# Output projection in paired 64-row pieces, constant matmuls in the opening, and another order of the opening loads

## The chip, the cores and the metric

The kernel runs on one core of one Trainium2 chip. The metric is the device time of one execution in microseconds, lower is better. The core has a matrix engine (TensorE, PE in the profile; its weight loads are listed apart as PEld), a vector engine (DVE), a scalar engine (ACT), GpSimd (POOL), and SyncE (SP), whose queue here issues every transfer (DMA). Matmul results go to PSUM, which has 8 banks of 512 fp32 columns.

## The reference, cut to what matters

```python
# x: (1, 2048, 576), bf16;  wqkv: (576, 1728);  wo: (576, 576)
# w_gate, w_up: (576, 4608);  w_down: (4608, 576)
xn = layernorm(x)
q, k, v = split(xn @ wqkv)                      # 32 heads of 18
p = softmax(where(0 <= i - j < 256, q @ k.T * 18 ** -0.5, -1e9))
s = (p @ v) @ wo                                # the output projection
h = sigmoid(xn @ w_gate) * (xn @ w_up)
out = x + s * silu(h @ w_down)
```

## The kernel before, in words

The 2048 tokens are worked in four chunks `c` of 512 (`CH`), each of four blocks of 128 (`QPC`). A chunk goes through these stages:

- `build_ln` loads the x blocks, normalises them (two `bn_stats`, `bn_aggr`, an add, a power on POOL, one `tensor_scalar`, a 64-column wrap copy) and turns them over into `xn`: in chunk 0 by PE transposes (L403, nine to a block) and an ACT copy (L412), in later chunks by DMA. The feature dimension of 576 lies there as nine slabs of 64, each in both halves of the 128 rows, in a shifted order, so that two matmuls of 64 rows can run side by side in the upper and the lower half of the array. The program calls this mode `r64`.
- `build_qkv` makes q, k and v of each block with `project` (L416): nine slabs by two halves, 18 matmuls of 288 columns (L423). The order in chunk 0 is the string `QKV_FIRST`. A q or k result is copied to a slot of `pk` (three slots, `RPK`) and turned over into `qkp` by a DMA transpose (`qkt`, L462); a slot is free again when that transpose has landed, so the fourth q or k projection waits for the first transpose, and so on.
- `build_attn` does the scores (L505), exponentials (L527), masks (L561) and p·v (L584) for eight groups of four heads. `after_pv` divides, turns over, and writes `op_`; DMAs named `oc` (L618 to L628) gather 18-row pieces of `op_` into `oT`, whose rows are the contraction of the output projection.
- `build_wo` (L630) is the output projection: per block five row tiles (four of 126 rows, one of 72), each against 512 and 64 columns of `wo_sb`: ten matmuls a block, 40 a chunk (L642), each block into its own pair of PSUM banks. ACT copies the result to `sat` (L650).
- `build_ffn`: gate and up, 36 tiles `ft` of 128 features (`fa`, `fb`: L678, `r64`, 18 matmuls of 512 columns each; the two last up-matmuls of a tile are carried into the next tile's `fa`), tanh on ACT (L664), product on DVE (L668). The weights come in groups of three tiles, four DMAs a group (`load9`), into a ring of three slots (`RW`). Then the down projection (L746 and, in the last block, L776): 128-row matmuls of 512 and 64 columns in turn, in pieces of four tiles `q`.

The order of every engine's program is computed by `schedule` (L819): a list scheduler takes, per engine, the operation with the smallest start time plus `prio` times 40 ns, by durations and a transfer model that are written in the source. Operations with `prio` 1 (projections, output projection) so go ahead of those with `prio` 3 (gate/up and down) where both can start. An operation that writes PSUM names candidate banks (`Psum`): the output projection pairs (4, 5), (6, 7), (0, 1), (2, 3); gate and up one bank each of 4 to 7; the down projection one of the same pairs. It can be placed only where all users of the earlier tenant have been placed. All transfers are issued by SP, in that static order, each behind its own waits. `emit` writes semaphore waits between engines; between two PE operations it writes none.

In chunk 0 SP issues the four x blocks, then 12 parts of `wqkv` (q, k, v, four each), three parts of the first gate/up group, three q/k transposes, the fourth part, and so on.

## Time and profile before

| what | value |
|---|---|
| median of 3 runs (lowest, highest) | 580.01 us (579.92, 580.15) |
| the profiled execution: time / span | 580.4 us / 578.4 us |
| PE busy in the span | 564.7 us (98%), 6185 matmuls |
| gate and up (L678) | 2592 matmuls, 299.4 us busy |
| down (L746) | 1080 matmuls, of which the trace has 1053 |
| q, k, v (L423) | 864 matmuls, 56.4 us busy |
| output projection (L642) | 160 matmuls: 64 of 126 rows by 512 columns, 64 of 126 by 64, 16 of 72 by 512, 16 of 72 by 64 |
| transposes of chunk 0 (L403) | 36 matmuls of 128 columns |
| first matmul | 6.75 us after the start of the span |
| DMA | 72.73 MB, 126 GB/s in the mean; 248 GB/s from 5 to 10 us, 236 from 10 to 15 us |

The span is the time from the first to the last instruction of the profiled execution; the 2.0 us to its own time lie around it. A matmul's duration in the profile runs from its start to a modelled end, and matmuls overlap: what one costs is the distance from its start to the next one's start. Rows of groups give durations; starts are read from the timeline.

### The profile page before, as it was taken

What the parts mean: (1) busy time and instruction counts of PE and PEld (TensorE: products, weight loads), DVE (VectorE), ACT (ScalarE), POOL (GpSimd) and SP (SyncE); (2) the same over time, 40 slices, a digit from 0 to 9 for tenths busy, and PEclk for the clock granted to TensorE, in tenths of its full rate; (3) what the DMA queues carried; (4) which work ended last, traced back from release to release, by engine and by line L of the source; (5) the groups of instructions that cost most, each with busy time, mean ns of one, the idle gap of its engine ahead of it and who ended that gap; (6) DMA issues with size and microseconds to landing.
All of it is one profiled execution on the core that took longest, in us unless ns stands there. A gap on an engine that the chain in (4) does not pass through costs nothing.

```text
span 578.4 us, 14464 instructions
## 1 busy us (share of the span) xinstructions
PE 564.7 (98%) x6185; PEld 274.1 (47%) x6212; DVE 295.0 (51%) x588; ACT 304.5 (53%) x411; POOL 25.0 (4%) x51
## 2 busy tenths in 40 slices
PE   5999999999999999999999999999999999999997
PEld 3654334457544444445754444444564444444554
DVE  4247988403157887611226697751312677774112
ACT  5357887214168787530337788732133878873101
POOL 3001110000000010000000011000000000000000
PEclk9999999999999999999999999999999999999999
DMA  8999999624946665313793556432389355651010
GB/s 202 203 191 231 216 223 199 160 44 92 210 93 134 145 155 127 80 44 82 106 210 92 139 132 158 111 90 46 69 167 185 73 124 136 134 126 39 1 42 20
DMA packets 124091, 72.73 MB, mean 126 GB/s; under 512 B 53157, under 2 KB 123525, under 8 KB 124029
## 3 DMA queue, kind: packets, MB, share of 16 engines
q1 hardware_dynamic: 124029, 71.82, 58.8%
q8 instruction: 49, 0.80, 0.6%
q14 instruction: 13, 0.11, 0.1%
HBM read 55.15 MB, written 2.36 MB: 99 GB/s over the span
## 4 chain that ended last, share of the span: by engine, by line
PE 97%; DVE 1%; DMA 1%; issue 0%; ACT 0%; SPq 0%
PE ps L678 50%; PE ps L746 23%; PE ps L423 9%; PE ps L505 5%; PE ps L584 4%; PE ps L642 3%; PE ps L776 2%; DMA xr<-in_A_x_dram 1%; PE ps L403 1%; ACT sat L650 0%; DVE bnst L367 0%; DVE bnst L369 0%; DVE xnr L380 0%; DVE mv L371 0%; SPq L193 0%
## 5 line engine op out<-in xcount | busy, mean ns | idle before, releaser
L678 PE MATMUL ps<-xn,wgs 64*128 64x512 bf16 x2592 | 299.4, 377 | 0.0
L527 ACT ACTIVATE expr<-ps 128x1024 bf16<-128x1024 f32 (+2 forms) x192 | 175.8, 968 | 39.9 <-PE ps L505 39.2
L678 PEld LDWEIGHTS ps<-xn,wgs 64*128 64x128 bf16 x2592 | 121.0, 94 | 148.5 <-issue 14.3
L746 PE MATMUL ps<-wd_sb,hT 128*128 128x64 bf16 (+1 forms) x1053 | 131.9, 284 | 2.5 <-issue 1.1
L668 DVE SCALAR_TENSOR_TENSOR hT<-tring,ps 128x512 bf16<-128x512 bf16 x144 | 97.2, 675 | 49.5 <-ACT tring L664 25.1
L664 ACT ACTIVATE tring<-ps 128x512 bf16<-128x512 f32 x144 | 86.3, 599 | 68.7 <-PE ps L678 66.0
L561 DVE TENSOR_TENSOR expr<-expr,m 128x1024 bf16<-128x1024 bf16 (+1 forms) x152 | 82.3, 572 | 60.4 <-ACT expr L527 60.2
L746 PEld LDWEIGHTS ps<-wd_sb,hT 128*128 128x128 bf16 x1080 | 68.1, 98 | 66.4 <-issue 4.4
L807 ACT ACTIVATE thf<-ps 128x576 bf16<-128x576 f32 (+2 forms) x17 | 10.6, 623 | 98.4 <-PE ps L746 90.8
L423 PE MATMUL ps<-wqkv_sb,xn 64*128 64x288 bf16 x864 | 56.4, 286 | 0.0
L809 DVE SCALAR_TENSOR_TENSOR thf<-thf,ps 128x576 bf16<-128x576 bf16 (+2 forms) x17 | 12.2, 719 | 85.4 <-ACT thf L807 85.4
L423 PEld LDWEIGHTS ps<-wqkv_sb,xn 64*128 64x128 bf16 x864 | 42.0, 95 | 13.0 <-issue 1.4
L505 PE MATMUL ps<-qkp 18*128 18x384 bf16 (+2 forms) x704 | 36.8, 276 | 0.0
L457 DVE CAST pk<-ps 128x576 bf16<-128x576 f32 x16 | 12.1, 757 | 48.0 <-PE ps L423 48.0
L599 DVE STREAM_TRANSPOSE tf<-ps 128x512 f32<-128x512 f32 x32 | 22.9, 716 | 13.5 <-PE ps L505 10.4
L505 PEld LDWEIGHTS ps<-qkp 18*128 18x128 bf16 x704 | 11.1, 92 | 34.6 <-issue 20.2
L458 ACT ACTIVATE pk<-ps 128x576 bf16<-128x576 f32 x16 | 10.4, 652 | 31.2 <-PE ps L423 31.2
L566 POOL COPY qkp<-qkp 128x256 bf16<-128x256 bf16 x24 | 12.2, 507 | 313.3 <-PE ps L505 313.3
L584 PE MATMUL ps<-expr,vau 128*32 128x256 bf16 (+2 forms) x704 | 25.6, 277 | 0.0
L613 DVE STREAM_TRANSPOSE op__63<-pk 128x512 bf16<-128x512 bf16 x32 | 22.7, 708 | 0.9 <-DVE pk L607 0.3
L642 PE MATMUL ps<-wo_sb,oT 126*128 126x512 bf16 (+3 forms) x160 | 20.4, 286 | 0.0
L584 PEld LDWEIGHTS ps<-expr,vau 128*32 128x32 bf16 x704 | 13.1, 96 | 15.4 <-ACT tring L664 7.6
(36 smaller groups left out, 141.1 us busy)
## 6 DMA issues: line engine op xcount, KB each, us to landing
wgs<-in_B_w_gate_dram SPq DMA_DIRECT2D x48, 240.0 KB, 3.9
wgs<-in_B_w_up_dram SPq DMA_DIRECT2D x48, 240.0 KB, 4.7
wgs<-in_B_w_up_dram SPq DMA_DIRECT2D x48, 192.0 KB, 4.2
wgs<-in_B_w_gate_dram SPq DMA_DIRECT2D x48, 192.0 KB, 4.8
wd_sb<-in_B_w_down_dram SPq DMA_DIRECT2D x9, 576.0 KB, 6.9
xf<-in_A_x_dram SPq DMA_DIRECT2D x18, 144.0 KB, 2.3
out_dram<-xf SPq DMA_DIRECT2D x15, 144.0 KB, 1.8
xr<-in_A_x_dram SPq DMA_DIRECT2D x14, 144.0 KB, 4.2
```

The lines of the kernel that those rows point to most:

```text
L423: r = e.matmul(self.bank(ps, HV, hf), self.xn[r0:r0 + 64, k, i * P:(i + 1) * P], self.wqkv_sb[r0:r0 + 64, j, k, :], start=(k == 0), stop=( ...
L505: r = e.matmul(self.ps[:, b:b + n * P], self.qkp[r0:r0 + DH, hg, k0:k0 + P], self.qkp[r0:r0 + DH, hg, q0 * P:(q0 + n) * P], start=True, st ...
L527: return e.activation(self.expr[:, es, 2 * pr:2 * pr + 2, 0:nblk * P], src, ACTF.Exp, scale=SM_SCALE)
L561: return e.tensor_tensor(ap, ap, m, ALU.mult)
L584: r = e.matmul(self.ps[32 * j:32 * j + 32, b + q0 * P:b + (q0 + n) * P], vf[:, v0:v0 + 32], self.expr[:, es, j, pos * P:(pos + n) * P], st ...
L599: t1 = self.rd("DVE", dve_ns(CH), lambda e, ps=ps: e.transpose(tf.rearrange("p g d -> p (g d)"), self.bank(ps)), f"t1:{c}:{hg}", deps=[o_p ...
L613: t2 = self.op("DVE", dve_ns(CH), lambda e, on=on: e.transpose(self.op_[:, hg % NOT, :], on.rearrange("p g d -> p (g d)")), f"t2:{c}:{hg}" ...
L642: r = e.matmul(self.ps[:, b + n0:b + n1], self.oT[0:k, kt, qi * P:(qi + 1) * P], self.wo_sb[0:k, kt, n0:n1], start=(kt == 0), stop=(kt == ...
L664: return e.activation(self.tring[:, st_, :], self.bank(ps), ACTF.Tanh, scale=0.5)
L668: return e.scalar_tensor_tensor(self.hT[:, ft, :], self.tring[:, st_, :], 1.0, self.bank(ps), ALU.add, ALU.mult)
L678: return e.matmul(self.bank((pg, pu)[gu][ft]), self.wgs[r0:r0 + 64, slots[ft // FG], i, fl * P:(fl + 1) * P], self.xn[r0:r0 + 64, i, :], s ...
L746: r = e.matmul(self.ps[:, b + n0:b + n1], lhsT, self.wd_sb[:, q, fl, n0:n1], start=(ft == 0), stop=(ft == NFT - 1))
```

## The change

Four things change together.

1. **Output projection.** `oT` and `wo_sb` now hold full tiles of 128 rows in the first four row tiles and the other 64 rows of the contraction in the fifth. In the fifth, the lower 64 rows carry token columns 0 to 255 and the upper 64 rows columns 256 to 511. The matmuls take 64 rows each and go in pairs, one in each half of the array, for two blocks at once: blocks 0 and 2, then 1 and 3. A pair of blocks takes two operations: the first has all five row tiles (20 matmuls), with one block's lower and the other's upper half; the second (16 matmuls, four row tiles) has the halves exchanged. The second adds to banks that the first wrote through the other half of the array, so it gets a real semaphore wait on the first (`fence`), also in the scheduler's model. Each operation holds two pairs of banks. The gather DMAs become 18-row pieces with a rest of 2 rows, and two 16-row pieces of 256 columns for each late head group: 16 `oc` issues a chunk in place of 11; the weight's small pieces become eight of 16 rows in place of four of 18.
2. **Opening on PE.** DVE fills a tile of `hT` with ones first of all; PE runs ten matmuls of 512 columns on it before any data has arrived, and one more after each of the transposes of blocks 0 and 1. Their bank (3) is not read.
3. **Loads.** SP's order in the opening becomes, by the new priorities: x0, x1, q weights, x2, v weights, x3, k weights, the first gate/up group. The layernorm of chunk 0 gets a higher priority for earlier blocks (`LN_STEP`), and the scheduler's estimate of the transfer time of `wqkv` goes from 1.55 to 1.35.
4. **Projections of chunk 0** follow `QKV_FIRST` in its new order, with v next to q. The first one (q0) is split after four slabs, so that its first part needs only the first half of `xn` and two of the four weight parts.

```diff
--- before.py
+++ after.py
...
 NOT = 4
-KO = 7 * DH
+WO_PRIO = 1
 KL = 4 * DH
...
 SKEW = 2
-QKV_FIRST = "q0 k0 q1 k1 q2 k2 q3 k3 v0 v1 v2 v3"
+QKV_FIRST = "q0 q1 v0 v1 q2 v2 k0 v3 k1 q3 k2 k3"
 QKV_NEXT = "q0 k0 q1 v0 v1 k1 q2 k2 v2 q3 k3 v3"
...
 LATE_SLACK = 5000.0
-LN_STEP = 0
+LN_STEP = 1
+WARM = 10
+X0_SLACK = 0.0
+WARM_MORE = (1, 1)
+X_PRIO = (-9, -9, -7, -5)
+QKV_LOAD = (-8, -4, -6)
+W0_PRIO = -3
+WARM_NS = 427.0
+W_FACTOR = 1.35
 XT_BYTES = 1.6
...
                 for o in self.ops:
-                    if o.name.startswith("wo:0:"):
+                    if o.name.startswith("wo:0:") and o.fence is None:
                         o.add_dep(self.op_wo)
...
         self.op_negh = op("DVE", 60, lambda e: e.memset(self.neghalf[:, :], -0.5), "neghalf", prio=0)
+        self.op_pre = op("DVE", 250, lambda e: e.memset(self.hT[:, 0, :], 1.0), "pre", prio=-9)
         id1 = op("POOL", 200, lambda e: e.memset(self.op_[:, NOT - 1, 0:P], 1.0), "id1", prio=0)
...
         self.op_vones = op("POOL", 300, lambda e: e.memset(self.vau[:, :, H, :], 1.0), "vpad", deps=[vo1], prio=1)
+        self.warm(WARM, "warm:0", [self.op_pre])
         self.op_pkz = op("ACT", 1300 + 1900, lambda e: e.memzero(self.pk[:, :, :, :]), "pkz", prio=0)
 
-    def load9(self, low, up, w_low, w_up, name, lane, deps, prio, eng="SP"):
+    def warm(self, n, name, deps, odeps=()):
+        ps = Psum((3,))
+
+        def f(e):
+            for k in range(n):
+                r = e.matmul(self.bank(ps), self.hT[:, 0, 0:P], self.hT[:, 0, :], start=True, stop=True)
+            return r
+        self.op_warm = self.pe(n * WARM_NS, f, name, deps=deps, prio=-9, psum=[ps], odeps=odeps)
+
+    def load9(self, low, up, w_low, w_up, name, lane, deps, prio, factor=1.55):
         cols = w_low.shape[1]
...
                                            (low[:, 5:NC, :], a[:, 1:NC:2, :], 4), (up[:, 4:NC, :], b[:, 0:NC:2, :], 5))):
-            out.append(self.dma(dst, src, 1.55 * n * 64 * cols * 2, f"{name}.{k}", lane + (k,), deps=deps, prio=prio,
-                                issue=W_ISSUE_NS, eng=eng))
+            out.append(self.dma(dst, src, factor * n * 64 * cols * 2, f"{name}.{k}", lane + (k,), deps=deps, prio=prio,
+                                issue=W_ISSUE_NS))
         return out
...
         self.op_wqkv = [None] * 3
-        for j, eng in ((0, "SP"), (1, "SP"), (2, "SP")):
+        for j in range(3):
             c0 = j * D
             self.op_wqkv[j] = self.load9(self.wqkv_sb[0:64, j, :, :], self.wqkv_sb[64:P, j, :, :], wq[:, c0:c0 + HV],
-                                         wq[:, c0 + HV:c0 + D], f"wqkv{j}", ("wqkv", j), [], -1 if eng == "ACT" else 0, eng)
+                                         wq[:, c0 + HV:c0 + D], f"wqkv{j}", ("wqkv", j), [], QKV_LOAD[j], W_FACTOR)
 
...
                      "wo0", ("wo", 0), deps=gate, prio=6),
-            self.dma(self.wo_sb[KL:KO, 0:4, :], wv[0:KO - KL, :, :], 4 * (KO - KL) * D * 2, "wo1", ("wo", 1), deps=gate,
+            self.dma(self.wo_sb[KL:P, 0:4, :], wv[0:P - KL, :, :], 4 * (P - KL) * D * 2, "wo1", ("wo", 1), deps=gate,
                      prio=6)]
-        for t in range(4):
-            self.op_wo.append(self.dma(self.wo_sb[t * DH:(t + 1) * DH, 4, :], wv[KO - KL:KL, t, :], DH * D * 2,
+        n = KL - (P - KL)
+        for t in range(8):
+            self.op_wo.append(self.dma(self.wo_sb[t * n:(t + 1) * n, 4, :], wv[P - KL:KL, t % 4, :], 2 * n * D,
                                        f"wo{2 + t}", ("wo", 2 + t), deps=gate, prio=6))
...
                            ("x", i if c == 0 else sx), deps=dx + ([self.op_f1[(c - 1, 6 + 3 * i)]] if c > 0 else []),
-                           prio=0 if c == 0 else 4, slack=DMA_SLACK_NS if c == 0 else LATE_SLACK)
+                           prio=X_PRIO[i] if c == 0 else 4, slack=X0_SLACK if c == 0 else LATE_SLACK)
             sb_, db_ = self.r_bn.take()
...
                     return e.activation(self.xn[:, i0:i0 + n, i * P:(i + 1) * P], src, ACTF.Copy)
+                if i < len(WARM_MORE) and i1 == NC:
+                    self.warm(WARM_MORE[i], f"warm:{i + 1}", [], [tr])
                 self.op_xn[i].append(self.rd("ACT", act_ns(n * P), f_xe, f"xe:{st}", deps=[tr], prio=pr, psum=[ps]))
...
 
-        def f(e):
-            for k in range(NC):
+        def f(e, k0, k1):
+            for k in range(k0, k1):
                 for hf in range(2):
...
             return r
-        o = self.pe(NC * mm_ns(HV), f, name, deps=self.op_xn[i] + self.op_wqkv[j] + deps, prio=1, psum=[ps], mode="r64",
-                    odeps=[after])
+        odeps = [after]
+        k0 = 0
+        if c == 0 and i == 0 and j == 0:
+            k0 = 4
+            odeps = [self.pe(k0 * mm_ns(HV), lambda e: f(e, 0, k0), name + ":0",
+                             deps=self.op_xn[i][:1] + self.op_wqkv[j][:2] + deps, prio=1, psum=[ps], mode="r64")]
+        o = self.pe((NC - k0) * mm_ns(HV), lambda e: f(e, k0, NC), name, deps=self.op_xn[i] + self.op_wqkv[j] + deps,
+                    prio=1, psum=[] if k0 else [ps], mode="r64", odeps=odeps)
+        if k0:
+            ps.users.append(o)
         self.r_xn.release(0, o)
...
         if half == 1:
-            self.op_oc[c][1].append(self.dma(
-                self.oT[g * DH:(g + 1) * DH, 4, :], self.op_[96:96 + DH, g, :], 2 * DH * CH * 2, f"oc:{c}:{hg}:s",
-                ("oc", 8 + g), deps=[t2] + wo_done, prio=-2, issue=820, slack=OC_SLACK))
+            n = KL - (P - KL)
+            for hf in range(2):
+                r0 = 64 * hf + g * n
+                cs = slice(hf * CH // 2, (hf + 1) * CH // 2)
+                self.op_oc[c][1].append(self.dma(
+                    self.oT[r0:r0 + n, 4, cs], self.op_[96 + DH - n:96 + DH, g, cs], n * CH * 2, f"oc:{c}:{hg}:s{hf}",
+                    ("oc", 8 + 2 * g + hf), deps=[t2] + wo_done, prio=-2, issue=820, slack=OC_SLACK))
         if g == NOT - 1:
-            for j in range(4 - half):
+            for j in range(4):
                 r0 = (4 * half + j) * DH
+                n = min(P - r0, DH)
                 self.op_oc[c][half].append(self.dma(
-                    self.oT[r0:r0 + DH, 0:4, :], self.op_[32 * j:32 * j + DH, :, :], 2.8 * DH * NOT * CH * 2,
+                    self.oT[r0:r0 + n, 0:4, :], self.op_[32 * j:32 * j + n, :, :], 2.8 * n * NOT * CH * 2,
                     f"oc:{c}:{hg}:{j}", ("oc", half * 4 + j), deps=self.op_on[c][hg - 3:hg + 1] + wo_done, prio=-2,
...
         self.op_wop = [None] * QPC
-        self.op_s = []
-        for qi in range(QPC):
-            ps2 = Psum((4, 5), (6, 7), (0, 1), (2, 3))
-            ss, ds = self.r_s.take()
-
-            def f_wo(e, ps2=ps2, qi=qi):
-                b = ps2.banks[0] * 512
-                for n0, n1 in ((0, 512), (512, D)):
-                    for kt in range(NKT):
-                        k = KO if kt < 4 else KL
-                        r = e.matmul(self.ps[:, b + n0:b + n1], self.oT[0:k, kt, qi * P:(qi + 1) * P],
-                                     self.wo_sb[0:k, kt, n0:n1], start=(kt == 0), stop=(kt == NKT - 1))
+        self.op_s = [None] * QPC
+        for pair in ((0, 2), (1, 3)):
+            ps2 = [Psum((4, 5), (6, 7), (0, 1), (2, 3)) for _ in pair]
+            slots = [self.r_s.take() for _ in pair]
+
+            def f_wo(e, swap, ps2=ps2, pair=pair):
+                for kt in range(NKT - swap):
+                    for n, (n0, n1) in enumerate(((0, 512), (512, D))):
+                        for hf in range(2):
+                            w = hf ^ swap
+                            r0 = 64 * hf
+                            qi = pair[w]
+                            r = e.matmul(self.bank(ps2[w], n1 - n0, n), self.oT[r0:r0 + 64, kt, qi * P:(qi + 1) * P],
+                                         self.wo_sb[r0:r0 + 64, kt, n0:n1], start=(swap == 0 and kt == 0),
+                                         stop=(swap == 1 and kt == NKT - 2), tile_position=(r0, 0))
                 return r
-            wo = self.pe(NKT * (mm_ns(512) + mm_ns(64)), f_wo, f"wo:{c}:{qi}",
-                         deps=self.op_oc[c][0] + self.op_oc[c][1] + self.op_wo + ds, prio=1, psum=[ps2])
-
-            def f_se(e, ps2=ps2, ss=ss):
-                b = ps2.banks[0] * 512
-                return e.activation(self.sat[:, ss, :], self.ps[:, b:b + D], ACTF.Copy, scale=0.25)
-            se = self.rd("ACT", act_ns(D), f_se, f"se:{c}:{qi}", deps=[wo], prio=2, psum=[ps2])
-            self.op_s.append((ss, se))
-            self.op_wop[qi] = wo
+            wa = self.pe(NKT * (mm_ns(512) + mm_ns(64)), lambda e, f=f_wo: f(e, 0), f"wo:{c}:{pair[0]}",
+                         deps=self.op_oc[c][0] + self.op_oc[c][1] + self.op_wo + [d for _, ds in slots for d in ds],
+                         prio=WO_PRIO, psum=ps2, mode="r64")
+            wo = self.pe((NKT - 1) * (mm_ns(512) + mm_ns(64)), lambda e, f=f_wo: f(e, 1), f"wo:{c}:{pair[0]}s",
+                         deps=[wa], prio=WO_PRIO, mode="r64")
+            wo.fence = wa
+            for ps in ps2:
+                ps.users.append(wo)
+            for qi, ps, (ss, _) in zip(pair, ps2, slots):
+                def f_se(e, ps=ps, ss=ss):
+                    b = ps.banks[0] * 512
+                    return e.activation(self.sat[:, ss, :], self.ps[:, b:b + D], ACTF.Copy, scale=0.25)
+                se = self.rd("ACT", act_ns(D), f_se, f"se:{c}:{qi}", deps=[wo], prio=2, psum=[ps])
+                self.op_s[qi] = (ss, se)
+                self.op_wop[qi] = wo
 
...
                     slots.append(sw)
-                    wp = fg + 1 if c == 0 and fg < RW else -2
+                    wp = (fg + 1 if fg else W0_PRIO) if c == 0 and fg < RW else -2
                     fc = slice(fg * FG * P, (fg + 1) * FG * P)
...
                 elif e == "PE":
-                    t = free[e]
+                    t = free[e] if s_.fence is not o else o.done + SEM_NS
                 else:
...
                     k, v = d.tok
-                    if e == "PE" and d.eng == "PE":
+                    if e == "PE" and d.eng == "PE" and d is not o.fence:
                         continue
...
```

More of the change, by code (lines that the diff above doesn't have):

```diff
@@ L99 @@
     __slots__ = ("eng", "occ", "lat", "deps", "fn", "name", "prio", "start", "done", "tok",
-                 "needs_tok", "nbytes", "idx", "slack", "succs", "cidx", "odeps", "alloc", "mode", "lane")
+                 "needs_tok", "nbytes", "idx", "slack", "succs", "cidx", "odeps", "alloc", "mode", "lane", "fence")
     def __init__(self, eng, occ, fn, name, deps, prio, nbytes=0, odeps=(), alloc=(), mode=None, lane=None):
@@ L122, in __init__ @@
         self.lane = lane
+        self.fence = None
     def add_dep(self, d):
```

## The prediction, made before the changed kernel was run

> **What bounds the kernel now.** I read the page's shares first, then the chain that ended last, then PE's and SP's timelines in the two places that the change touches.
>
> ```profile
> PE 564.7 (98%) x6185; PEld 274.1 (47%) x6212; DVE 295.0 (51%) x588; ACT 304.5 (53%) x411; POOL 25.0 (4%) x51
> ...
> PEclk9999999999999999999999999999999999999999
> DMA  8999999624946665313793556432389355651010
> ...
> PE 97%; DVE 1%; DMA 1%; issue 0%; ACT 0%; SPq 0%
> ```
>
> PE is the chain. After its first matmul it hardly ever waits, so an edit is worth what it changes in PE's sequence, as long as nothing feeds PE later than now. The DMA row shows nines up to 100 us: while chunk 0 runs, transfers have no room to spare. PEclk, all nines, can't be trusted for the first slice: the trace's first clock record, at full speed, stands at 12.96 us. PE's timeline of the opening, with start, duration and count:
>
> ```profile
> 6.75 1.14 PE L403 MATMUL ps<-op__63,xnr 128*128 128x128 bf16 x9 [6.75 <-DVE xnr L384]
> 8.08 2.10 PE L403 MATMUL ps<-op__63,xnr 128*128 128x128 bf16 x18 [0.19 <-DVE xnr L384]
> 10.12 2.34 PE L423 MATMUL ps<-wqkv_sb,xn 64*128 64x288 bf16 x18
> 12.39 0.93 PE L403 MATMUL ps<-op__63,xnr 128*128 128x128 bf16 x9
> 13.25 10.10 PE L423 MATMUL ps<-wqkv_sb,xn 64*128 64x288 bf16 x162
> 23.20 8.79 PE L678 MATMUL ps<-xn,wgs 64*128 64x512 bf16 x79
> ```
>
> Up to 12.9 us a transpose starts every 107 ns, afterwards every 56; a pair of projection matmuls takes 240 ns in the first projection and 122 in the later ones: PE runs at half speed until then. From 13.25 on it is full: nine projections (1.11 us each), then gate/up from 23.20 on. Two of the twelve projections are left; they run inside gate/up at 31.6 to 35.5 us. SP's queue tells why gate/up begins at 23.20:
>
> ```profile
> 10.73 0.62 SPq L193 DMA_DIRECT2D wgs<-in_B_w_gate_dram  x1
> 11.39 0.62 SPq L193 DMA_DIRECT2D wgs<-in_B_w_up_dram  x1
> 12.05 0.63 SPq L193 DMA_DIRECT2D wgs<-in_B_w_gate_dram  x1
> 13.29 5.55 SPq L192 DMA_TRANSPOSE qkp<-pk  x3
> 18.88 0.60 SPq L193 DMA_DIRECT2D wgs<-in_B_w_up_dram  x1
> ...
> 24.16 7.65 SPq L192 DMA_TRANSPOSE qkp<-pk  x3
> 31.86 0.60 SPq L193 DMA_DIRECT2D wgs<-in_B_w_up_dram  x1
> ```
>
> The fourth part of the first group is issued at 18.88, behind three transposes that hold the queue 5.55 us. By the semaphore events its parts land at 15.28, 16.13, 16.89 and 22.95. The second group lands from 24.06 to 27.04 us, the third's last part at 35.83.
>
> The output projection in chunk 1 (chunks 2 and 3 look the same):
>
> ```profile
> 238.81 11.83 PE L678 MATMUL ps<-xn,wgs 64*128 64x512 bf16 x108
> 250.57 5.10 PE L642 MATMUL ps<-wo_sb,oT 126*128 126x512 bf16 x40
> 255.60 0.60 PE L678 MATMUL ps<-xn,wgs 64*128 64x512 bf16 x2
> 256.37 1.39 PE L746 MATMUL ps<-wd_sb,hT 128*128 128x64 bf16 x10 [0.16 <-ACT sat L650]
> ```
>
> The wait on `sat` is no wait: the down projection's weights load at 256.14, and its first 512-column matmul lacks a record (the trace has 1053 of 1080). Single starts give what I need: a 512-column step 216 ns, a 64-column step 29 to 31 (the weight load hidden in both), a pair of 64-row halves 216 with the halves 3 to 4 ns apart. Where `r64` and full-array work meet, 92 to 98 ns come on top (last gate/up start to first L642 start 308 instead of 216; L642 to L678, and L746 to L423, 125 instead of 29).
>
> **The output projection, part by part.** Now: 20 x (216 + 30) = 4.93 us a chunk, 19.7 in all. After: nine pair-steps for each two blocks, so 18 x (216 + X), where X is a pair of 64-column matmuls. X isn't in the trace. Lower bound 30 (the halves overlap, as the 512s do), upper 61 (one after the other, each with its weight load). I take 33, nearer to what 288 and 512 columns show in halves: 4.48 us a chunk, **1.8 us saved** in all; at 61 it would be 4.99, 0.2 lost.
>
> What it adds is changes of mode. In chunks 1 to 3 L642 sits between gate/up and its last two matmuls: three changes up to the down projection. In chunk 0 it sits inside the down projection (113.9 to 119.0 us), all full-array: no change beyond the one into that stage. The new pieces are `r64`, and each needs two of four bank pairs. One pair is the down projection's (two in chunk 0), so the second two blocks must wait for two `sat` copies of 0.65 us, and the down projection runs meanwhile. Between first and second piece stands the fence, by the scheduler's constants 166 + 50 ns after the end: a down piece with `prio` 3 costs it 120 ns and goes first. Also the gather comes later: one small and one 2-row issue more behind the last head group, about 1.5 us of SP time, and the projection was placed just as gate/up ended; I expect its first piece at that end, and the other three alone inside the down projection. So seven changes in place of three in chunks 1 to 3, eight more in chunk 0: 20 x 94 ns = **1.9 us added**. If the fence is sat out instead, a 64-column matmul's recorded 193 ns against its 29-ns step plus the 50 give 0.2 us, the price of the two changes that it spares. Bounds: all pieces beside gate/up, -0.6 us; every piece alone, +2.2. The extra issues on SP (5 a chunk by 0.82 us or less) lie in stretches where SP waits; without that cover they delay a gather by their own length.
>
> The page "TensorEngine Tiling (Array Packing)", Key Properties, speaks against the change: a change of tiling mode drains the engine. The trace agrees that a change costs. Taken as a drain of the whole recorded latency (380 less 216, 164 ns), the 20 changes would cost 3.3 us and not 1.9; I stay with the measured distance.
>
> **The opening, part by part.** The x1 block lands at 4.38 now and issues no later after; the layernorm of block 0 still passes through it (static DVE order), so the first transposes stay near 6.7 us. The ten constant matmuls run from 1.2 us (after one DVE fill of about 0.3) at 240 x 512 / 288 = 427 ns, to 5.5: PE is idle there now, so they cost nothing; if x came before 5.5 they would delay it. The two later ones cost 0.2 to 0.4 us each in a stretch that waits for ACT and loads.
>
> Issue stays at 0.66 us a part, and the bytes land at 236 GB/s (162 KB every 0.69 us). Without x2 and x3 ahead the q weights land about 0.95 earlier, by 7.7; x2 8.1, the v weights by 11.1, x3 11.6, the k weights by 14.2 as the last part now, and the fourth part of the first group, no longer behind transposes, at 16.89 + 0.9 = **17.8**. PE: q0 and q1 by 10.7 (four ACT copies of 0.6 to 0.7 set that), third transposes at 10.7, then v0, v1, q2, v2, v3 from 11.1 (5 x 1.11) and the last transposes (0.65): done at 17.3. The fourth q/k projection must wait for the first `qkt` to land (now 19.24), so gate/up starts at 18.0 and the five others go inside it. Like with like: now 23.20 + 2 x 1.11 = 25.4; after 18.0 + 5 x 1.11 = 23.6: **1.85 us saved**. Bounds: 2.5 if only projections count (22.9), nothing if what follows is late.
>
> Next in line are the second group, due at 18.0 + 5.85 + 3 x 1.11 = 27.2, landing about 25.5 (one part less ahead than now: -0.9, and the rest as now), and the third, due near 35.8, landing about 34.9. It is close, but I count no wait.
>
> The page "TensorE: Matmul & The Clock Gate", Part 1, lets the full clock come after a busy window of 3.4 us. By its rule the ten matmuls (4.27 us) could raise it before the first transposes. Whether they do, no row here shows.
>
> **Sum.** -1.85 - 1.8 + 1.9 = -1.75 us. Against the profiled 580.4 this is 578.65; that execution lies 0.4 over the median, so I predict **578.3 us**. A difference under 0.2% (1.16 us) is about what a measurement of this kernel can't tell from none.
>
> **Rivals.**
> 1. *Few changes of mode* (chance 0.20): the pieces stand in twos, and the added changes go. For it: the scheduler may find banks. Against: two pairs are held. 580.0 - 1.85 - 1.8 = 576.4.
> 2. *The 64-column halves don't overlap* (0.18): X = 61. For it: no short matmul in halves is in the trace. Then -1.85 + 0.2 + 1.9 = +0.25: 580.3.
> 3. *The clock isn't raised* (0.08): the constant tile does nothing and PE stays at half speed to about 12.9. What then lies on the path is v0, v1 and what follows 11.1: some 0.7 us past 17.8: 579.0.
> 4. *Slower: the transposes get ahead of the second group* (0.12). With q projected first, three `qkt` are ready by 15 us, and k's have `prio` 0 against 2 for the group. If three more go out ahead of its parts, 7.65 us of SP by the row above, it lands at 33.1 against 27.2: about 5.9 us of wait, 584. It decides from a landing 1.75 us past 27.2, at 29.0, on. Against: the slot ring holds the k projections back to 20 us.
>
> My forecast has 0.42; its own range is 577.4 to 579.2. The 80% range takes in rivals 1 to 3 and leaves most of 4 out: **576.2 to 580.8**. Faster by over 0.2% (under 578.85): 0.9 of the forecast, rival 1, half of rival 3: 0.62. Within: 0.26. Slower: rival 4, 0.12.
>
> **What would show it.** Right: first gate/up start at 18.0, five projections inside it; paired matmuls 3 to 4 ns apart with 64-column pair-steps near 33 ns; PE's time from the first to the last output projection matmul broken by down pieces, with steps of about 95 ns on top at each. Wrong: gate/up later than 19, gaps in gate/up of chunk 0 that end with a landing, 64-column pair-steps near 60, or pieces of the output projection back to back.

## The result, and the profile after

| kernel | median us (lowest to highest, runs) | ratio to before, 95% interval | profiled: time / span us |
|---|---|---|---|
| before | 580.09 (579.46 to 580.73, 20) | | 580.4 / 578.4 |
| changed | 578.88 (578.24 to 579.72, 20) | 0.998 [0.9973, 0.9987] | 579.1 / 577.1 |

The change takes off 1.21 us; 578.3 was predicted. The page of the changed kernel, busy shares, clock and DMA rows, and the chain of waits by engine:

```profile
PE 568.1 (98%) x6352; PEld 273.9 (47%) x6352; DVE 296.2 (51%) x589; ACT 303.3 (53%) x411; POOL 24.4 (4%) x51
...
PEclk9999999999999999999999999999999999999999
DMA  8999889634956664342693656544179356551010
...
PE 95%; DMA 2%; SPq 2%; DVE 1%; issue 0%; POOL 0%; ACT 0%
```

PE still is the chain, but DMA and SP's queue have risen from 1% and 0% to 2% each, 4% of 577 us or some 23 us together. That is the opening, which now follows loads, as PE's timeline of it shows (start, duration, count, idle time before and its releaser):

```profile
1.50 4.26 PE L327 MATMUL ps<-hT 128*128 128x512 bf16 x10 [1.50 <-DVE neghalf L304]
6.09 0.68 PE L424 MATMUL ps<-op__63,xnr 128*128 128x128 bf16 x9 [0.32 <-DVE xnr L405]
...
7.63 2.56 PE L446 MATMUL ps<-wqkv_sb,xn 64*128 64x288 bf16 x36
10.82 0.68 PE L424 MATMUL ps<-op__63,xnr 128*128 128x128 bf16 x9 [0.63 <-DVE xnr L405]
11.43 2.38 PE L446 MATMUL ps<-wqkv_sb,xn 64*128 64x288 bf16 x36
15.37 0.68 PE L424 MATMUL ps<-op__63,xnr 128*128 128x128 bf16 x9 [1.56 <-DVE xnr L405]
...
19.40 1.88 PE L723 MATMUL ps<-xn,wgs 64*128 64x512 bf16 x15
...
24.46 1.69 PE L723 MATMUL ps<-xn,wgs 64*128 64x512 bf16 x14 [0.32 <-ACT pk L489]
26.31 1.28 PE L446 MATMUL ps<-wqkv_sb,xn 64*128 64x288 bf16 x18 [0.17 <-DMA qkp<-pk]
```

The constant matmuls run at 427 ns each, and the clock record at full speed now stands at 5.46 us (12.96 before): the first nine transposes go at 56 ns and not 107. But PE waits: by its starts 0.79 us before 10.82, 1.72 before 15.37, 0.48 before 24.46, 0.33 before 26.31. Gate/up begins at 19.40 (23.20 before, behind three projections more); yet the first scores, behind the same twelve projections and the same 106 gate/up matmuls, start at 37.495 against 37.145. The opening has become no shorter: it ends 0.35 us later. SP's queue, where a row is one issue or several (x2), with how long they held the queue:

```profile
13.01 0.62 SPq L202 DMA_DIRECT2D wgs<-in_B_w_up_dram  x1
13.67 5.36 SPq L201 DMA_TRANSPOSE qkp<-pk  x2
19.07 0.62 SPq L202 DMA_DIRECT2D wgs<-in_B_w_gate_dram  x1
19.73 0.62 SPq L202 DMA_DIRECT2D wgs<-in_B_w_up_dram  x1
20.39 1.33 SPq L201 DMA_TRANSPOSE qkp<-pk  x1
```

The first gate/up group is issued as planned, its last part at 13.01. By the semaphore events its parts land at 15.76, 18.15, 18.52 and 19.27: the second comes 2.4 us behind the first, where before the first three came 0.8 us apart (15.28, 16.13, 16.89). The transposes of q0 and q1 are issued at 13.67 and 15.25, ahead of this gap; but before has transposes at 13.29 and 15.36 too, just as close behind its second and third part, and there the parts land on pace. What the changed kernel's trace has ahead of its gap, and the one of before has not, is one packet of 16 KB, on the queue that the profile calls "instruction", from 14.90 to 16.17 us; before has it at 17.18 to 18.20, when its three parts have landed. The DMA view of 14.5 to 16.5 us has it in the row of its queue (packets, MB, share of 16 engines); below that are the rates of the DMA view from 17.6 to 19.6 us, in slices of 0.05:

```profile
q8 instruction: 1, 0.02, 4.0%
```

```profile
GB/s 174 184 159 143 159 138 97 82 56 46 61 36 31 15 31 15 15 31 15 31 15 21 15 20 15 20 15 20 15 148 292 287 302 282 297 287 287 282 232 307
```

4.0% of 16 engines for 2 us is one engine for 1.28 us. From 18.25 to 19.05 us the core moves about 15 GB/s, a sixteenth of the 236 that it moved from 10 to 15 us in before: by this estimate one DMA engine is behind and the others wait.

Gate/up starts 0.13 us after the last landing. But PE would have come to it at 19.30 at the earliest: its last projection ahead of gate/up starts its last matmul at 19.175, and a step is 122 ns. So the late landing and the late layernorm of the fourth block end within 0.1 us of each other.

The output projection of chunk 1, PE's timeline (before: 40 matmuls in 5.10 us, three changes of mode):

```profile
239.48 11.83 PE L723 MATMUL ps<-xn,wgs 64*128 64x512 bf16 x108
251.15 0.38 PE L680 MATMUL ps<-wo_sb,oT 64*128 64x512 bf16 x1
251.15 0.38 PE L723 MATMUL ps<-xn,wgs 64*128 64x512 bf16 x1
...
251.39 4.76 PE L680 MATMUL ps<-wo_sb,oT 64*128 64x512 bf16 x70
256.09 6.27 PE L791 MATMUL ps<-wd_sb,hT 128*128 128x512 bf16 x49
```

All four pieces stand back to back, and the two last up-matmuls of gate/up run beside the first piece, in the other half of the array (251.149 and 251.152 us). From one step (216 ns) after gate/up's last start ahead of the projection to the start of the down projection it is 4.94 us, where it was 5.66 (250.476 to 256.139, the latter from the down projection's first weight load): 0.73 less. Chunks 2 and 3 show the same. In chunk 0 the pieces stand apart:

```profile
110.30 4.09 PE L791 MATMUL ps<-wd_sb,hT 128*128 128x512 bf16 x32
114.32 1.40 PE L680 MATMUL ps<-wo_sb,oT 64*128 64x512 bf16 x20
115.65 1.16 PE L791 MATMUL ps<-wd_sb,hT 128*128 128x512 bf16 x8
116.74 1.15 PE L680 MATMUL ps<-wo_sb,oT 64*128 64x512 bf16 x16
117.83 2.13 PE L791 MATMUL ps<-wd_sb,hT 128*128 128x512 bf16 x16
```

Two more pieces follow in the same way. From the down projection's start to the next chunk's first projection it is 23.01 us against 22.68 before (from 109.945, where the first down matmul must have started, 0.308 after gate/up's last; its record is missing): 0.33 more.

The account by the two traces: +0.35 in the opening, +0.33 in chunk 0, 3 x -0.73 in chunks 1 to 3: -1.51, and the last matmul starts at 572.381 against 573.895, -1.51. Behind it the span goes on for 4.75 us against 4.46, which gives 0.3 of it back; the span is 1.2 shorter.

### The profile page after: what moved, and what is told of

Its sections match the earlier page's. It is cut to its first block, busy times and chain, and to the rows that moved or that the text cites. A ratio compares the mean times of both kernels' runs of the same rounds, so it can differ in the third digit from the quotient of the medians.

```text
span 577.1 us, 14818 instructions
## 1 busy us (share of the span) xinstructions
PE 568.1 (98%) x6352; PEld 273.9 (47%) x6352; DVE 296.2 (51%) x589; ACT 303.3 (53%) x411; POOL 24.4 (4%) x51
## 4 chain that ended last, share of the span: by engine, by line
PE 95%; DMA 2%; SPq 2%; DVE 1%; issue 0%; POOL 0%; ACT 0%
PE ps L723 50%; PE ps L791 23%; PE ps L446 8%; PE ps L536 5%; PE ps L615 4%; PE ps L680 3%; PE ps L821 2%; SPq L202 1%; DMA qkp<-pk 1%; DMA xf<-in_A_x_dram 1%; DVE pk L488 0%; SPq L201 0%; PE ps L424 0%; POOL rstd L397 0%; DVE bnst L388 0%
## 5 line engine op out<-in xcount | busy, mean ns | idle before, releaser
L723 PEld LDWEIGHTS ps<-xn,wgs 64*128 64x128 bf16 x2592 | 119.7, 94 | 150.1 <-issue 15.1
L791 PE MATMUL ps<-wd_sb,hT 128*128 128x512 bf16 (+1 forms) x1080 | 135.8, 287 | 0.0
L536 PEld LDWEIGHTS ps<-qkp 18*128 18x128 bf16 x704 | 11.1, 92 | 34.6 <-issue 20.2
L695 ACT ACTIVATE sat<-ps 128x576 bf16<-128x576 f32 x16 | 9.2, 654 | 21.5 <-PE ps L680 21.5
```

The costliest lines, as they stand in the source:

```text
L536: r = e.matmul(self.ps[:, b:b + n * P], self.qkp[r0:r0 + DH, hg, k0:k0 + P], self.qkp[r0:r0 + DH, hg, q0 * P:(q0 + n) * P], start=True, st ...
L723: return e.matmul(self.bank((pg, pu)[gu][ft]), self.wgs[r0:r0 + 64, slots[ft // FG], i, fl * P:(fl + 1) * P], self.xn[r0:r0 + 64, i, :], s ...
L791: r = e.matmul(self.ps[:, b + n0:b + n1], lhsT, self.wd_sb[:, q, fl, n0:n1], start=(ft == 0), stop=(ft == NFT - 1))
```

## The experiments

Each kernel was timed beside runs of before on the same chip; those had medians of 580.00 to 580.15 us. Run 1 is labelled e1 and so on; where a label's number differs it is given.

| run | median us (lowest to highest, runs) | ratio to before, 95% interval |
|---|---|---|
| 1 projection alone | 578.51 (577.82 to 579.68, 7) | 0.9974 [0.9963, 0.9985] |
| 2 opening alone | 580.34 (579.55 to 581.84, 10) | 1.0006 [0.9997, 1.0016] |
| 3 changed, no constant matmuls | 578.34 (577.68 to 579.49, 8) | 0.9974 [0.9964, 0.9984] |
| 4 before, with constant matmuls | 579.68 (579.11 to 581.26, 10) | 0.9995 [0.9985, 1.0005] |
| 5 chunk 0's projection later | 578.65 (578.13 to 578.98, 9) | 0.9974 [0.9964, 0.9984] |
| 6 gather assumed later | 582.41 (581.88 to 582.82, 5) | 1.0039 [1.0025, 1.0052] |
| 7 all x first | 578.84 (577.83 to 579.36, 10) | 0.9979 [0.9969, 0.9988] |
| 8 first gate/up group early too | 577.55 (576.97 to 578.75, 6) | 0.9959 [0.9946, 0.9971] |
| 9 second group early too (e10) | 580.89 (577.30 to 585.93, 10) | 1.0016 [0.9982, 1.0050] |
| 10 as 8, no constant matmuls (e11) | 578.24 (577.42 to 579.54, 9) | 0.9967 [0.9957, 0.9977] |
| 11 as 9, no constant matmuls (e12) | 578.07 (576.85 to 579.86, 10) | 0.9965 [0.9953, 0.9978] |
| 12 as 9, once more (e13) | 578.32 (577.57 to 581.66, 12) | 0.9979 [0.9964, 0.9993] |

### Runs 1 and 2: each half of the change alone

Run 1 gives the changed kernel the opening of before:

```diff
-QKV_FIRST = "q0 q1 v0 v1 q2 v2 k0 v3 k1 q3 k2 k3"
+QKV_FIRST = "q0 k0 q1 k1 q2 k2 q3 k3 v0 v1 v2 v3"
...
-LN_STEP = 1
+LN_STEP = 0
...
-X0_SLACK = 0.0
+X0_SLACK = 600.0
...
-X_PRIO = (-9, -9, -7, -5)
-QKV_LOAD = (-8, -4, -6)
-W0_PRIO = -3
+X_PRIO = (0, 0, 0, 0)
+QKV_LOAD = (0, 0, 0)
+W0_PRIO = 1
...
-W_FACTOR = 1.35
+W_FACTOR = 1.55
...
-        self.warm(WARM, "warm:0", [self.op_pre])
...
-        if c == 0 and i == 0 and j == 0:
+        if False:
```

Run 2 keeps the new opening and takes the output projection, its gather and its weight's loads from before (40 full-array matmuls a chunk, one operation a block).

> The output projection in paired pieces, with the whole opening (loads, order, constant matmuls, split q0) as before. Theory P (from the two traces: the projection gains, the opening loses): each of chunks 1 to 3 gains 0.73 us, chunk 0 loses 0.33, so 580.1 - 1.85 = 578.2, faster than the changed kernel. Rival O (as predicted: mode changes eat what the pairs gain): +0.1, 580.2. The pieces stand back to back in chunks 1 to 3, and a 512+64 pair-step takes 248 ns (P), or they are broken up by down pieces (O).

> The opening's edits alone, the output projection as before. Theory P: first attention scores 0.35 us later than before, so 580.1 + 0.35 = 580.4. Rival O: -1.85, 578.2.

Run 1 is 1.6 us faster than before, run 2 0.2 slower with an interval of -0.2 to +0.9; together -1.4, the changed kernel's -1.2. The whole gain is the projection's, and the opening brings nothing that these runs can tell. The prediction had it the other way round. Run 1's first scores start at 36.635, and its opening is that of before, which has 37.145 in its own trace: an opening varies by half a microsecond from one execution to the next. The +0.35 read above is within that; the medians of run 2 are the better measure.

### Runs 3 and 4: the constant matmuls

Run 3 is the changed kernel without them, run 4 the kernel before with them and nothing else.

```diff
-        self.op_pre = op("DVE", 250, lambda e: e.memset(self.hT[:, 0, :], 1.0), "pre", prio=-9)
...
-        self.warm(WARM, "warm:0", [self.op_pre])
...
-                if i < len(WARM_MORE) and i1 == NC:
-                    self.warm(WARM_MORE[i], f"warm:{i + 1}", [], [tr])
```

> The changed kernel without the matmuls on the constant tile and without its fill. If the loads and the late normalisation of the fourth block set the end of the opening (theory P), PE's half speed falls into waits that are there anyway: first gate/up still at about 19.4 us, 578.9 to 579.5. If PE's speed set it, the 2.7 us of half speed come back: 581.6. The clock should then be seen full at 9 to 13 us instead of 5.46.

> The kernel before with the constant tile and its matmuls alone. If PE's half speed is what the opening of before loses, all 2.7 us come: 577.4. If the first gate/up group's landing (22.95 us) holds PE, only what the earlier transposes pull that landing forward: 579.0 to 579.8.

PE's timeline of run 3:

```profile
6.11 2.10 PE L422 MATMUL ps<-op__63,xnr 128*128 128x128 bf16 x18 [6.11 <-DVE xnr L403]
8.14 4.26 PE L442 MATMUL ps<-wqkv_sb,xn 64*128 64x288 bf16 x36
12.33 0.68 PE L422 MATMUL ps<-op__63,xnr 128*128 128x128 bf16 x9
12.94 3.48 PE L442 MATMUL ps<-wqkv_sb,xn 64*128 64x288 bf16 x54
...
19.41 1.88 PE L719 MATMUL ps<-xn,wgs 64*128 64x512 bf16 x15
```

The first two projections take 4.26 us in place of 2.56: half speed, which ends at 12.02 us by the clock's record. Ahead of 19.41 only 0.2 us of waiting is left, and gate/up starts at the same time to 0.01 us, since the group's last part lands at 19.274 here and at 19.267 there. The half speed fills time in which PE would have waited for loads. The median is 0.5 us below the changed kernel's, with overlapping intervals, and also below both expectations; in the trace the third transpose goes out at 19.06 in place of 20.39, and the first scores start at 36.747, 0.75 earlier. In run 4 the other way round: the first gate/up goes from 23.20 to 20.23, 3 us earlier, but 2.2 of it only because two projections more now run inside gate/up, and ahead of it PE waits 0.96 and 0.68 us for parts of `wqkv`. The first scores come 0.75 us earlier, and of that 0.4 shows in the median, with an interval that holds zero. What the constant matmuls do to the clock is plain; to the time they do nothing that these runs can tell.

### Runs 5 and 6: where the pieces stand

Run 5 lets chunk 0's projection follow a late tile of the next chunk's stage; run 6 lets the scheduler assume that the gather DMAs take 3 us longer.

```diff
                     if o.name.startswith("wo:0:") and o.fence is None:
                         o.add_dep(self.op_wo)
+                        o.odeps.append(self.f2_ops[(1, NWD - 1)])
```

```diff
-OC_SLACK = 3000.0
+OC_SLACK = 6000.0
```

> The changed kernel, with the output projection of chunk 0 put behind the first two blocks of its down projection. Its four pieces then stand together next to the q, k, v projections of chunk 1, in the same mode, and chunk 0 has no added change of mode; chunk 1's pieces are broken up twice by it, four changes more. If a change costs what the trace shows (94 ns) and that is all: -8 x 0.094 + 4 x 0.094 = -0.4 us, 578.5. If the loss of chunk 0 has another cause (the fence, waits for banks), no gain: 578.9.

> The changed kernel with the scheduler's slack for the gather at 6 us instead of 3: in chunks 1 to 3 the four pieces then stand alone inside the down projection, as the prediction took it, nine changes of mode a chunk against one. If 94 ns a change is the price: 3 x 8 x 0.094 = +2.3 us and some 0.15 for the two carried matmuls that no longer run beside a piece: 581.3. If the position costs nothing: 578.9.

In run 5 chunk 0's pieces do stand together, 139.04 to 143.43 us, beside the next projections, which are 64-row work too. But chunk 1's, placed after them in the schedule, now break up: two of them stand alone inside the down projection, four changes more than in the changed kernel. Half of what one place gains is lost at the other, and the 0.2 us left can't be told from nothing. Run 6 makes what the prediction had assumed for chunks 1 to 3. PE's timeline of its chunk 1:

```profile
251.42 3.12 PE L791 MATMUL ps<-wd_sb,hT 128*128 128x512 bf16 x24
254.46 1.40 PE L680 MATMUL ps<-wo_sb,oT 64*128 64x512 bf16 x20
255.79 1.15 PE L791 MATMUL ps<-wd_sb,hT 128*128 128x512 bf16 x8
256.88 1.15 PE L680 MATMUL ps<-wo_sb,oT 64*128 64x512 bf16 x16
```

The last matmul of each piece and the first of the next stage are 121 to 125 ns apart where 29 is a step within it: 92 to 96 ns a change. From gate/up's end to the next chunk's projections it costs 0.85 us over the changed kernel, eight changes more: 0.75 by that price. The whole run is 3.5 us slower and not 2.4 as expected, since chunks 2 and 3 cost 1.29 each: there attention, too, ends elsewhere in the schedule (its last matmul of chunk 2 at 387.04 us in place of 379.75), and the 0.44 a chunk that this adds stays open. By the price alone, three chunks with eight changes each are 2.3 us: that the pieces stand together is worth more than the 1.2 that the whole change brings.

### Runs 7 and 8: the order of the loads

The longer of the two waits for the layernorm, the one at 15.37, is explained by the chain of waits (start, duration, what):

```profile
7.75 4.45 DMA xf<-in_A_x_dram
...
13.04 0.66 DVE pk L488
...
14.08 0.56 POOL rstd L397
...
14.67 0.44 DVE xnr L401
15.13 0.19 DVE xnr L405
```

The last x block is issued at 7.75 behind q and v weights and lands at 12.20; from there its layernorm takes 3.1 us more on DVE and POOL, with a copy of a projection between. Run 7 loads all four x blocks before any weights; run 8 adds to it that the first gate/up group goes ahead of the v and k weights.

```diff
-X_PRIO = (-9, -9, -7, -5)
+X_PRIO = (-9, -9, -9, -9)
...
-W0_PRIO = -3
+W0_PRIO = -7
```

> The changed kernel with all four x blocks loaded first, then q, v, k weights. It takes away the waits of PE at 10 and 13.6 us for the normalisation of blocks 2 and 3 (0.8 and 1.7 us). If the landing of the first gate/up group (19.27 us) sets the end of the opening, the waits come back ahead of it: first gate/up still at 19.2 to 19.6, time 578.5 to 579.2. If the late x blocks set it: some 1.7 us less, 577.2.

> As x_first, and the first gate/up group loaded second, ahead of the v and k weights. If transfers in order of need set the opening, gate/up starts at about 12 us (0.59 + 0.66 + 0.88 MB at 236 GB/s after 2.2 us) and PE has work from then on: first attention scores 1 us or more earlier than in the changed kernel (37.5), time 577.4 to 578.2. If the sum of bytes up to the second and third group sets it, the wait moves there: no gain, 578.9.

In run 7 both waits are gone, and PE waits for other transfers instead: gate/up 1.56 us for its group, to 18.73, then a projection 1.28 us for a q/k transpose, to 24.58. The time is that of the changed kernel to 0.04 us. The waits for the layernorm were not what alone bound the opening. Run 8 takes the load that was last and puts it ahead of eight parts of `wqkv`; its parts land 0.7 to 1.0 us apart, the last at 12.43. PE's timeline:

```profile
10.51 2.38 PE L446 MATMUL ps<-wqkv_sb,xn 64*128 64x288 bf16 x36
12.85 2.53 PE L723 MATMUL ps<-xn,wgs 64*128 64x512 bf16 x20
15.13 7.97 PE L446 MATMUL ps<-wqkv_sb,xn 64*128 64x288 bf16 x126
22.86 3.69 PE L723 MATMUL ps<-xn,wgs 64*128 64x512 bf16 x32
27.82 6.00 PE L723 MATMUL ps<-xn,wgs 64*128 64x512 bf16 x54 [1.26 <-DMA wgs<-in_B_w_up_dram]
```

One wait is left, for the second group, whose fourth part lands at 27.57, 2.5 us behind the third (1.64 us from start to start, 1.42 over a step). The first scores start at 37.03, which is 0.46 earlier than in the changed kernel and not the 1 us that was expected, but behind ten more gate/up matmuls (1.08 us). Gate/up of chunk 0 ends at 108.44 in place of 109.99, and the kernel beats both: 1.3 us under the changed one, 2.6 under before. Its interval, 0.9946 to 0.9971, ends below the changed kernel's own, though only just.

### Runs 9 to 12: the last wait, and the constant matmuls again

Runs 9 and 12 are one kernel: run 8 with the second gate/up group ahead of the k weights. Run 10 is run 8 and run 11 is run 9 without the constant matmuls (the edit of run 3).

```diff
-                    wp = (fg + 1 if fg else W0_PRIO) if c == 0 and fg < RW else -2
+                    wp = (W0_PRIO, -5, 3)[fg] if c == 0 and fg < RW else -2
```

> The kernel with all four x blocks and the first gate/up group ahead of the v and k weights (577.55 us) still has one wait of 1.64 us on PE in the opening, for the second gate/up group. Here that group goes ahead of the k weights as well. If loads set the opening, most of that wait goes: 576.2 us (576.0 to 576.8), no gap over 0.5 us in gate/up of chunk 0. Rival: four parts more ahead of the k weights (4 x 0.69 = 2.8 us later) only move the wait to the k projections or to the first scores: 577.5 us, with a gap of 1 to 2 us before a k projection or the scores.

> The kernel of 577.55 us without the constant matmuls. There PE had no wait between its first transposes and the second gate/up group. If the constant matmuls pay as soon as loads no longer hide half speed, the clock is full at about 12 us in place of 6.99, the 27 later transposes cost 51 ns more each (1.4 us), the first pairs of projection matmuls about 115 ns more each (27 pairs, 3 us, less what is waited for anyway): the first gate/up start at 15 in place of 12.85 and, since the wait of 1.64 us for the second group takes up part of it, 578.0 to 579.0 us. Rival: the constant matmuls are worth nothing in any order of the loads, as they were in the changed kernel: 577.0 to 577.6 us.

> The order of loads with the second gate/up group ahead of the k weights, without the constant matmuls. If half speed was hidden behind the second group's landing before, it is not hidden here: 1 to 2 us over the same order with the constant matmuls. If the constant matmuls are worth nothing: within 0.5 us of it.

> The kernel with the second gate/up group ahead of the k weights once more, to see where its executions of 581 to 586 us lose 3 to 8 us against 577.3 (the mean granted clock of the slowest was 0.993 to 0.996 in place of 0.999). If the throttle takes the clock to half speed for a while, two times 0.6% of 576 us, about 7 us, stand in the clock row as a slice under full speed, and the matmuls of that stretch take about twice as long. If a transfer of the opening lands late in such executions, the clock row stays full, a gap of 3 us or more stands ahead of gate/up or the scores before 45 us, and the first projection of chunk 1 starts at 135 or later in place of 132.1. If the scatter belonged to that one chip, all executions stay within 577 to 579 us.

The wait for the second group goes, and others come. PE's timeline of run 12:

```profile
13.09 2.53 PE L723 MATMUL ps<-xn,wgs 64*128 64x512 bf16 x20 [0.28 <-issue]
15.79 4.59 PE L446 MATMUL ps<-wqkv_sb,xn 64*128 64x288 bf16 x72 [0.16 <-DMA wqkv_sb<-in_A_wqkv_dram]
...
25.28 2.38 PE L446 MATMUL ps<-wqkv_sb,xn 64*128 64x288 bf16 x36 [1.02 <-DMA qkp<-pk]
```

1.02 us of idle time now end with a q/k transpose (1.4 us from start to start; run 9 has 1.5 before the projections that follow gate/up's first 20 matmuls, for a part of `wqkv`). That is the rival's case: the wait has moved. What nobody expected is the scatter, 577.3 to 585.9 us in run 9 and 577.6 to 581.7 in run 12, where runs 8, 10 and 11 stay within 3 us. Four executions of run 9 at 583 to 586 had a mean granted clock of 0.993 to 0.996, the one at 581.7 in run 12 had 0.996; but those between 580.3 and 581.0 had 0.998 to 1.000. The executions whose traces there are took 577.97 and 578.86 and show a full clock row, so clock or late landing could not be told apart: the cause stays open. It is not that one chip's: run 12 was on its own.

Run 10 lies 0.7 us above run 8, with overlapping intervals; 578.24 is in the range expected if the constant matmuls pay. Its gate/up starts at 13.50 and not at 15, since the clock is full at 9.39 us there and not at 12 (6.99 in run 8, with gate/up at 12.85), and the distance of starts at the wait for the second group shrinks from 1.64 to 1.22 us; the last matmul starts at 571.07 against 570.84. Run 11 lies under both runs of its counterpart. So the constant matmuls are worth 0.7 us by the medians in one order of the loads and less than nothing in the other; whether they are worth anything where PE follows its loads closely stays open.

## Why the prediction was right, and where it was wrong

The total was right, the division was not: the opening came out 2.2 us worse than its term and the changes of mode 1.7 us better, and that the two misses cancel is luck. By the signs that the prediction named itself it was wrong twice: gate/up later than 19 (19.40), and pieces of the output projection back to back. Both sides by step:

| term of the sum | predicted | by the traces |
|---|---|---|
| opening | -1.85 | +0.35 (by the medians of run 2, +0.2) |
| paired matmuls | -1.8 | -2.0 |
| changes of mode | +1.9 | +0.2 |
| sum | -1.75 | -1.5, and -1.2 after the last stores |

**The opening, wrong.** Like with like, gate/up at 19.40 and not at 18.0 takes 1.40 from the 1.85, and two waits behind it take another 0.81: that makes +0.36, and +0.35 was measured. Three steps failed.

- "The fourth part of the first group, no longer behind transposes, at 16.89 + 0.9 = 17.8": the part was issued ahead of the transposes, but it landed at 19.27. Until then the landings were well told: q weights 7.38 (7.7 predicted), x2 8.18 (8.1), v weights 11.24 (11.1), x3 12.20 (11.6), k weights 14.73 (14.2). The 2.4 us between the group's first and second part are what no term held. That transposes issued behind a load hold it up doesn't explain this gap, since before has such transposes and no such gap. A packet of the instruction queue stands ahead of it; no run takes that packet away, so the cause stays open.
- The last transposes of the layernorm were put straight behind the projections, "done at 17.3", with no price for a layernorm that takes 3.1 us after x3. PE waited 1.7 us for it and was free for gate/up at 19.30. Run 7, where PE is free at 17.2, shows that this alone cost nothing.
- "I count no wait" for what comes next: there were two, 0.48 us, which ends with ACT's copy of a projection (23.75 to 24.40), and 0.33 for the third transpose, which went out at 20.39 behind two parts of the second group and landed at 26.27, 2.5 us behind the landing ahead of it. Again such a packet, from 24.05 to 25.04, stands ahead of it.

The prediction also read before's queue as the reason for gate/up at 23.20. The part that it names landed 0.25 us earlier, and PE went from the projections to gate/up in 128 ns, a plain step: PE had no wait there.

Where the earlier clock went can be summed. Half speed cost before 27 x 51 ns in the first transposes, 9 x 118 in the first projection and 0.25 in the last transposes: 2.7 us; 0.45 went in one wait at 7.6, and the first transposes now start 0.67 earlier. That is 3.8 us of gain. Against it stand waits of 0.79, 1.72, 0.48, 0.33 and a small one of 0.16, 3.5 in all, two constant matmuls among the transposes (0.43) and two or three more changes of mode (0.1 each): some 4.2. What PE gained in speed it spent in waits, which is what loads as the bound look like; run 3 says the same from the other side. There is one thing more: with the constant matmuls the first instruction packet comes earlier, at 14.90 against 16.24 (run 3), 14.35 in run 4 against 17.18 in before, and 14.04 in run 8 against 17.95 in run 10, and so among loads that are still under way.

**The paired matmuls, right.** A pair-step of 512 and 64 columns takes 245 to 248 ns: 216 and 29 to 31, so X was 29 to 31 where 33 was taken. 18 x 0.245 against 20 x 0.246 is 0.51 us a chunk and 2.0 in all. (The 0.73 of chunks 1 to 3 is this and two changes of mode less.) Rival 2 (halves that don't overlap, 61 ns) falls.

**The changes of mode, wrong in number.** Their price was right (92 to 96 ns against 94). The step that failed is "I expect its first piece at that end, and the other three alone inside the down projection": it holds in chunk 0, where eight changes came as predicted (+0.33 = 0.75 - 0.51, and 0.09), and in none of the other chunks, where one change is left of the three that before had (3 x -2 x 0.094 = -0.56, and +0.75 in chunk 0, make the 0.2). The reason given for it was the banks. But the second pair's first piece needs the last banks of gate/up and not the down projection's, and gets them just in time: the last product on DVE ends at 252.674 us, and that piece starts at 252.73. It also stands between a first piece and its fence, so that the fence costs nothing. The scheduler could do so since the gather came early enough in its model; run 6 takes this away and has the pieces apart in chunks 1 to 3, for 3.5 us, 2.3 of them by the price of the changes. Rival 1 gave 0.20 to just this; with an opening that had gained as well, it would have been its 576.4.

**Rivals 3 and 4.** The clock was raised, so 3 falls; run 3, where it comes as late as before, is no slower. Rival 4's mechanism is there in small: two transposes hold SP for 5.36 us between the first and the second group. The second group was due at 27.2 on PE and its last part landed at 28.38, but the third transpose and ACT had by then delayed PE too, and no wait for it is seen.

## What to carry to other kernels

Where an opening waits for loads, first order the loads by who needs them first, then look at PE's speed: constant matmuls that bring the full clock 7 us earlier gave nothing that these runs can tell, and one load moved ahead of two others gave 1.3 us. Before a late landing is put down to a neighbour in the queue, look whether another order of the same transfers, or the trace of before, has the neighbour without the delay, and what else moved on the DMA engines. When an operation is split into pieces that use the array in another way, count where a scheduler will put them, by bank and by the time its inputs come in its model: here 8 changes of mode a chunk, or one, hang on that placing, and decide between a gain and a loss. An early start of a stage is no gain until the next thing that it needs has been timed as well.

## What the runs showed of the hardware

- **Behind a packet of the instruction queue a landing comes late.** In the first 30 us of each of the 14 traces two such packets of 16 KB pass, each 1.0 to 1.8 us long, and 0.8 to 2.3 us after the end of each a transfer lands 1.6 to 3.0 us behind the one before it:

  | trace | first packet, us | late landing (the one before it) | first transpose issued |
  |---|---|---|---|
  | before | 17.18 to 18.20 | 19.24, a transpose (16.89) | 13.29 |
  | changed | 14.90 to 16.17 | 18.15 (15.76) | 13.67 |
  | run 3 | 16.24 to 17.51 | 19.27 (17.41) | 13.67 |
  | run 8 | 14.04 to 15.32 | 16.89 (14.99) | 13.37 |
  | run 9 | 13.41 to 14.67 | 15.88 (14.16) | 17.12 |
  | run 10 | 17.95 to 18.96 | 19.99, a transpose (17.70) | 13.38 |
  | run 11 | 18.35 to 19.66 | 21.36 (19.52) | 16.02 |
  | run 12 | 14.29 to 15.59 | 17.72 (15.65) | 16.69 |

  Transposes do not account for it: in run 9 the late part lands before any is issued, and in before and in run 10 all loads ahead of the packet land on pace with transposes issued behind them. The one wait of run 8 follows its second packet (24.11 to 25.42; landing 27.57). No run moved or removed a packet alone, so the order in time is shown, and the cause is not.
- **Halves of the array work for different stages at once.** A gate/up matmul in one half and one of the output projection in the other start 3 ns apart (251.149 and 251.152 us), and each half keeps its step of 216 ns.
- **The full clock came 3 to 6 us after PE's first matmul, and varies.** With constant matmuls from 1.5 us the record stands at 4.55 to 6.99 us in the traces of these kernels; without them, from first matmuls at 6.1 to 6.8, at 9.39 to 12.96. The Trainium skill, "TensorE: Matmul & The Clock Gate", Part 1, calls the number of matmuls before it variable from run to run, because the window of activity runs freely; the traces agree, with 3.2 us after the first transpose in run 10 and 5.9 in run 3, which run the same first 18 matmuls without a gap.
- **A change of mode costs 92 to 96 ns, not a full drain of a matmul's recorded latency** (164 ns, the other price that was weighed): in run 6 eight more of them cost 0.85 us in chunk 1, 106 ns each with all that comes along.
